# Seven products for one more pair in six tiles, strided units in halves, output products in another order

## The chip, the cores and the metric

The kernel runs on one core of one Trainium2 chip. The metric is device time in microseconds (us). In this text PE is TensorE's matmul stream, PEld its weight loads, DVE is VectorE, ACT is ScalarE, POOL is GpSimd and SP is SyncE. The program is scheduled by hand: each engine works through its own instructions in the order in which the kernel writes them, and semaphores tie the engines together.

## The reference, cut to what matters

Eight heads of attention feed a gated layer without an activation:

```
q, k, v: [8 batches, 8 heads, 576 positions, 64]
scores  = q k^T / 8
heads 0-3 keep 0 <= row - col < 32                      (local)
heads 4-7 keep row >= col and row % 32 == col % 32      (strided)
attn    = softmax(scores) v                             -> x: [8*576 tokens, 512]
a = x w_a ; b = x w_b                                   w_a, w_b: [512, 1536]
out = (a * b) w_out                                     w_out: [1536, 512]
```

Inputs and output are float32; the matmuls take bf16 and accumulate in float32.

## The kernel before, in words

**Tiles and slots.** The 4608 tokens are cut into nine tiles of 512, t = 0 to 8. (The short title of the change counts them from 1: its "tiles 3 to 7" are t = 2 to 6 here, and its "tile 8" is t = 7.) A tile has 16 slots. Slots 0 to 11 each make one of the twelve blocks of 128 hidden features: f = 0 to 11, or in pairs g = 0 to 5 with f = 2g and 2g + 1. Slots 12 to 15 are the output stage, which multiplies the hidden block `pf` by `w_out` and stores. While tile t runs, attention of batch b = t + 1 is threaded between its matmuls, at places that the tables STEPS, LATER, PAIRED, IN_P and IN_Y name. A table entry holds a position in the tile and what happens there: S0 to S7 (or s0 to s7 and m0 to m7, exponent and mask apart) are the scores of unit u = 0 to 7, V0 to V7 their products with v, Q0 to Q3 copies of q, O and I the way of the local heads through memory into `xT`. Units 0 to 3 are local heads, units 4 to 7 strided ones. `xT` is the attention output transposed, the right-hand side of the first matmuls; it holds four batches.

**A plain pair** (`ffn_ab`, L625): per block f, four matmuls of 512 columns for `a` and four for `b`; ACT copies `a` out (L646), DVE multiplies it by `b` into `pf` (L649).

**A pair by seven products** (`a_pair_mid` for t = 2 to 6, `a_pair` for t = 7 and 8): the `a` half of a pair is a two-by-two block product (two halves of the inner dimension, two blocks of features, two halves of the tokens), made of seven products instead of eight, each two matmuls of 256 columns. They work on sums of weights (`wsum_a`, DVE, L668) and of tokens (`xsum`, DVE, L678). ACT copies five results (L721, L724, L726, L731, L738), DVE adds three (L717). The `b` half stays at eight matmuls of 512 columns. The pair takes two slots; the first half of it ends at the first `yield`. Its order on PE, by the names in the code, is Y, X, three of b1, X again ("6"), Z ("7"), the last of b1 | X ("5"), Z ("4"), four of b0, X ("3"). After the bar comes the second slot. Steps listed at a slot's number are issued right behind that slot's matmuls. On DVE the second slot issues two additions, the step of IN_P, the third addition, then the two multiplies into `pf` (L714).

**The output stage** (`y_plan`, L895) uses the same seven-product form: fourteen groups of six matmuls of 256 columns, 84 in all, in the order Y_ORDER. A group is called by product and half, "60" for product 6 and half 0. Products 7, 6, 5 and 3 need sums over the hidden block, `ps` (`fast_s`, L829; n = 2, 1, 0, 3 in this order), which DVE makes from `pf`. ACT copies banks into `y_sb` (L860, L866), DVE adds (L858, L862, L864).

**PSUM banks.** From t = 2 on: three for `mm` and one for `tp` (dealt in turn by `mm_bank`), two for the scores `st`, one `o`, one `e`. `o` takes V0 to V3, and `o` and `e` together took the strided units 4 to 7. A bank can be written again only when its reader is done. For V0 to V3 the reader is DVE: a reciprocal (L468) and the normalising multiply (L486). For strided units (`step_VT`, L519 to L534) ACT makes the reciprocal of the row sums as exp(-ln) (L531, L532), then DVE multiplies into `xT` (L534).

**What is where before, in tiles 2 to 6.** Pairs 1 to 4 are by seven products, pairs 0 and 5 plain. V3 stands behind pair 3 (slot 7), S5's scores behind the first half of pair 4 (slot 8), V4 behind pair 4 (slot 9), S6's scores in pair 5, V5 behind it; S7, V6, V7 and the copies Q0, Q1 for the next batch lie in the output stage. In t = 7 pairs 1 to 5 are by seven products, in t = 8 all six.

Of the kernel before, what the change touches and what calls it, by code (L numbers as in the profile page):

```python
# [16 lines left out]
RS = 8  # L17
# [8 lines left out]
LV = 80  # L26
WCH = (0, 2, 5, 9, 12)
FAST_Y = (1, 2, 3, 4, 5, 6, 7, 8)
MID_A = {t: (1, 2, 3, 4) for t in (2, 3, 4, 5, 6)}
FAST_A = {7: (1, 2, 3, 4, 5), 8: (0, 1, 2, 3, 4, 5)}  # L30


@with_exitstack
def kernel(
# [473 lines left out]
    def step_VT(b, u):  # L508

        c, half, M, n, G = unit(u)  # L510
        p = ps.pop((b, u))
        if "e" in psum4:
            o = [psum4[nm].tile([128, 512], F32, tag=nm, name=nm) for nm in "oe"]
        else:
            o2 = psum4["o"].tile([128, 2, 512], F32, tag="o", name="o")
            o = [o2[:, j] for j in range(2)]
# [7 lines left out]
        if "e" not in psum4:  # L524
            by_j = lambda t: t.rearrange("d j (i p) -> d p i j", p=NP)
            nc.scalar.activation(by_token(r), by_j(o2[64:, :, :W]), ACT.Ln)
            nc.scalar.activation(r, r, ACT.Exp, scale=-1.0)
            nc.vector.tensor_mul(by_token(dst), by_j(o2[:64, :, :W]), by_token(r))
            return
        for j in range(2):  # L530
            nc.scalar.activation(by_token(r)[:, :, :, j], o[j][64:, :W].rearrange("d (i p) -> d p i", p=NP), ACT.Ln)  # L531
# [34 lines left out]
    def F_mm(f, w, kk):  # L566
# [115 lines left out]
    def a_pair_mid(t, g):  # L682
# [136 lines left out]
    def fast_s(t, n, gs):  # L819
        if t not in pss:  # L820
            pss[t] = nat.tile([128, FG * 5 * SW], BF16, tag="shared", name="ps").rearrange("p (n g m) -> p n g m", g=FG, n=5)
        s = pss[t][:, :, gs, :HT]
        x = pfs[t].rearrange("p (g e) (i m) -> p e i g m", e=2, i=2)[:, :, :, gs]
        a, b, op = ((x[:, 0, 1], x[:, 1, 1], ALU.add), (s[:, 0], x[:, 0, 0], ALU.subtract),
                    (x[:, 0, 0], x[:, 0, 1], ALU.subtract), (x[:, 1, 0], s[:, 1], ALU.subtract))[n]
        if (t, n) == (NT - 1, 2) and {gs.start, gs.start + 1} <= set(FAST_A[t]):
            later[t, gs.start] = lambda: nc.gpsimd.tensor_tensor(s[:, n], a, b, op=op)
            return
        nc.vector.tensor_tensor(s[:, n], a, b, op=op)  # L829
# [36 lines left out]
            nc.scalar.copy(part(0, 1), bank)  # L866
# [13 lines left out]
    def y_plan(t):  # L880

        plan, y = products(t), y_bufs()
        late = t in FAST_A
        if late:
            bank = {x: bank_of(nm, [128, 2, HN]) for x, nm in (("X", "mm"), ("Z", "mm"), ("Y", "tp"))}
        else:
            bank = {x: mm_bank([128, 2, HN]) for x in "ZXY"}

        def store_half(i):
            rows = out[TTOK * t:TTOK * (t + 1)].rearrange("(a i s q) c -> a s i (q c)", i=2, s=8, q=2)  # L890
            nc.sync.dma_start(out=rows[:, :, i], in_=y[i].rearrange("p q c -> p (q c)"))

        for k, q, g in by_block(Y_ORDER, 2 if late else 0):
            b, lhs, rhs = plan[k]
            nc.tensor.matmul(bank[b][:, q], lhsT=lhs(g, q), rhs=rhs(g), start=k in "172" and q == 0 and g == 0,  # L895
                             stop=g == FG - 1, skip_group_check=True)
# [54 lines left out]
    def ffn_y(t, j, mid):
        pf = pfs[t]
# [33 lines left out]
    with tc.manual_schedule(engines={ENG.PE, ENG.SP, ENG.Pool, ENG.DVE, ENG.Activation}):  # L986
# [76 lines left out]
        for t in range(NT):  # L1063
            slots += [(ffn_ab, t, f) for f in range(FD)] + [(ffn_ys if t in FAST_Y else ffn_y, t, j) for j in range(4)]
        for b in range(1, B):
            for pos, names in (STEPS.get(b) or {16 * (b - 1) + x: n for x, n in (PAIRED if b - 1 in MID_A else LATER).items()}).items():
                steps.setdefault(pos, []).append((b, names.split()))
            if b not in STEPS:
                for g in MID_A.get(b - 1, ()):
                    steps["p", b - 1, g] = [(b, IN_P[g].split())]  # L1070
                for n, names in IN_Y.items():
                    steps["y", b - 1, n] = [(b, names.split())]
# [107 lines left out]
```

## Time and profile before

| | us |
|---|---|
| three runs of the kernel | 318.88, 319.57, 321.58; median 319.57 |
| the profiled execution, its own time | 318.67 |
| its span (first to last instruction) | 317.0 |
| PE busy | 308.2 (97%) |
| DVE busy | 263.7 (83%) |
| ACT busy | 198.3 (63%) |
| POOL busy | 112.0 (35%) |
| one tile of t = 2 to 6, first to first matmul (tile 3: 123.05 to 155.93) | 32.88 |

The profiled execution spent 1.67 us outside its span. "Busy" of an engine joins overlapping instructions. A matmul of 512 columns is drawn as 0.38 us long, but the next one starts about 0.217 us later; so waits on PE are read from the distance of starts, not from gaps between bars. A timeline row merges equal instructions: its first number is the start of the first one, its second the time to the end of the last one, "x4" their number. A few matmul records are missing from the trace, and a row with fewer matmuls than the code issues has the same distance to the next row.

### The profile page before, as it was taken

What the parts mean: (1) busy time and instruction counts of PE and PEld (TensorE: products, weight loads), DVE (VectorE), ACT (ScalarE), POOL (GpSimd) and SP (SyncE); (2) the same over time, 40 slices, a digit from 0 to 9 for tenths busy, and PEclk for the clock granted to TensorE, in tenths of its full rate; (3) what the DMA queues carried; (4) which work ended last, traced back from release to release, by engine and by line L of the source; (5) the groups of instructions that cost most, each with busy time, mean ns of one, the idle gap of its engine ahead of it and who ended that gap; (6) DMA issues with size and microseconds to landing.
All of it is one profiled execution on the core that took longest, in us unless ns stands there. A gap on an engine that the chain in (4) does not pass through costs nothing. (4 is left out here: it accounts for less than half of the span.)

```text
span 317.0 us, 7353 instructions
## 1 busy us (share of the span) xinstructions
PE 308.2 (97%) x2770; PEld 220.6 (70%) x2798; DVE 263.7 (83%) x594; ACT 198.3 (63%) x414; POOL 112.0 (35%) x186
## 2 busy tenths in 40 slices
PE   7899999999999999999999999999999999999994
PEld 6754565455866687767999986769676966786684
DVE  6887876698979998999799978997899768847862
ACT  7964776455766776567666765686667755435541
POOL 8935712772263164115421434133101112203520
PEclk9999999999999999999999999999999999999999
DMA  9999999999799999999999999899352040004004
GB/s 159 168 205 202 203 184 202 216 104 172 127 137 148 223 144 81 127 228 134 108 114 225 118 130 106 202 138 134 30 154 58 0 135 0 2 0 133 2 0 134
DMA packets 127059, 40.32 MB, mean 127 GB/s; under 512 B 114864, under 2 KB 124144, under 8 KB 126832
## 3 DMA queue, kind: packets, MB, share of 16 engines
q0 software_dynamic: 79760, 19.20, 65.2%
q1 hardware_dynamic: 47120, 20.59, 38.8%
q8 instruction: 22, 0.36, 0.5%
q14 instruction: 13, 0.11, 0.1%
q10 hardware_dynamic: 144, 0.07, 0.1%
HBM read 38.93 MB, written 18.28 MB: 181 GB/s over the span
## 5 line engine op out<-in xcount | busy, mean ns | idle before, releaser
L625 PE MATMUL mm<-xT,wb_sb 128*128 128x512 bf16 (+1 forms) x189 | 46.8, 361 | 0.4
L625 PE MATMUL mm<-xT,wa_sb 128*128 128x512 bf16 (+1 forms) x183 | 46.1, 360 | 0.2
L1146 POOL CAST pace<-pf 1x1 f32<-1x1 bf16 x46 | 14.5, 316 | 81.1 <-DVE pf L714 31.6
L399 ACT ACTIVATE p<-st 72x576 bf16<-72x576 f32 (+1 forms) x56 | 36.4, 650 | 9.1 <-PE st L379 8.2
L709 PE MATMUL mm<-xT,wb_sb 128*128 128x512 bf16 (+1 forms) x160 | 38.0, 342 | 0.4
L646 ACT COPY a_sb<-mm 128x512 f32<-128x512 f32 x44 | 25.7, 583 | 15.7 <-PE mm L625 14.9
L895 PEld LDWEIGHTS <-ps 128*128 128x128 bf16 x336 | 32.7, 98 | 3.7
L625 PEld LDWEIGHTS <-wb_sb 128*128 128x128 bf16 x192 | 18.2, 98 | 16.8 <-DVE pf L714 0.3
L895 PE MATMUL mm<-wf,ps 128*128 128x256 bf16 x252 | 29.8, 273 | 0.0
L860 ACT COPY y_sb<-mm 128x512 f32<-128x512 f32 (+1 forms) x32 | 17.9, 558 | 19.0 <-PE mm L895 16.4
L649 DVE TENSOR_TENSOR pf<-a_sb,mm 128x512 bf16<-128x512 f32 x34 | 23.1, 680 | 5.9 <-ACT a_sb L646 5.8
L625 PEld LDWEIGHTS <-wa_sb 128*128 128x128 bf16 x192 | 17.4, 98 | 12.4
L1146 POOL COPY pace<-y_sb 1x1 f32<-1x1 f32 x22 | 8.4, 380 | 49.9 <-DVE y_sb L858 27.3
L895 PEld LDWEIGHTS <-pf 128*128 128x128 bf16 x252 | 23.5, 98 | 2.7
L775 PE MATMUL mm<-xT,wb_sb 128*128 128x512 bf16 x83 | 25.3, 379 | 0.1
L709 PEld LDWEIGHTS <-wb_sb 128*128 128x128 bf16 x192 | 18.7, 97 | 7.4
L238 POOL DMA_DIRECT2D vs<-in_v_dram x24 | 21.7, 907 | 3.9 <-ACT y_sb L860 1.3
L714 DVE TENSOR_TENSOR pf<-a_sb,mm 128x512 bf16<-128x512 f32 x35 | 22.7, 683 | 0.5
L895 PE MATMUL mm<-wo_sb,pf 128*128 128x256 bf16 x168 | 21.8, 273 | 0.0
L829 DVE TENSOR_TENSOR ps<-pf 128x512 bf16<-128x512 bf16 (+2 forms) x37 | 17.8, 481 | 0.7
L460 PEld LDWEIGHTS <-p 128*128 128x128 bf16 (+1 forms) x256 | 12.9, 97 | 5.2 <-DVE p L417 1.3
L417 DVE TENSOR_TENSOR p<-p,mask_l 128x576 int16<-128x576 int16 x32 | 14.4, 451 | 2.2 <-ACT p L399 2.0
(222 smaller groups left out, 734.2 us busy)
## 6 DMA issues: line engine op xcount, KB each, us to landing
out_dram<-y_sb SPq DMA_DIRECT2D x14, 512.0 KB, 4.8
kr<-in_k_dram POOLq DMA_DIRECT2D x12, 288.0 KB, 6.1
qr<-in_q_dram POOLq DMA_DIRECT2D x12, 288.0 KB, 8.1
vl<-in_v_dram POOLq DMA_DIRECT2D x6, 384.0 KB, 6.9
out_dram<-y_sb SPq DMA_DIRECT2D x7, 256.0 KB, 4.3
vs<-in_v_dram POOLq DMA_DIRECT2D x24, 72.0 KB, 5.7
xd<-xl SPq DMA_DIRECT2D x12, 144.0 KB, 4.0
wo_sb<-in_moe_w_out_dram POOLq DMA_DIRECT2D x4, 384.0 KB, 11.7
```

The lines of the kernel that those rows point to most:

```text
L238: nc.gpsimd.dma_start(out=vs_buf[b % 2][:, h, :, 0:D], in_=v[b, HL + h].rearrange("(p r) d -> p r d", r=RS))
L399: nc.scalar.activation(p_flat(p)[:M, :2 * W].rearrange("p (i n) -> p i n", n=2 * n), st[:M].rearrange("p a (i n) -> p (a i) n", n=256)[:, ...
L625: nc.tensor.matmul(ps_[:, c0:c0 + n], lhsT=w[:, kk, 128 * f:128 * (f + 1)], rhs=xT[:, kk, x0:x0 + n], start=(kk == first and c0 == 0), sto ...
L646: nc.scalar.copy(a_sb, ab[0])
L649: nc.vector.tensor_mul(pf[:, f, :].rearrange("p (i a s) -> p a i s", i=2, s=16), halves(a_sb), halves(ab[1]))
L709: nc.tensor.matmul(dst, lhsT=wb_sb[:, kk, 128 * f:128 * (f + 1)], rhs=rhs, start=kk == 0 and k in (None, 0), stop=kk == KD - 1 and k in (N ...
L714: nc.vector.tensor_mul(pf[:, 2 * g + e, :].rearrange("p (i a s) -> p a i s", i=2, s=16), halves(a[e]), halves(bank))
L775: nc.tensor.matmul(got[e], lhsT=wb_sb[:, kk, 128 * f:128 * (f + 1)], rhs=xT[:, kk, x0:x0 + TTOK], start=kk == 0, stop=kk == KD - 1)
L829: nc.vector.tensor_tensor(s[:, n], a, b, op=op)
L860: nc.scalar.copy({"1": part(0, 0), "7": part(0, 1), "6": part(1, 0), "5": part(1, 1)}[k], bank)
L895: nc.tensor.matmul(bank[b][:, q], lhsT=lhs(g, q), rhs=rhs(g), start=k in "172" and q == 0 and g == 0, stop=g == FG - 1, skip_group_check=True)
L1146: nc.gpsimd.tensor_copy(pace, done)
```

## The change

* In t = 2 to 6 pair 5 is made by seven products too, in t = 7 pair 0. Weight sums for group 5 are made together with those of groups 1 to 4.
* The strided units 4 to 7 of batches 3 to 7 are split by the parity of the positions. A half (`VT_p`) is four matmuls into one bank; one Ln and one Exp over 288 columns (`VT_x`) and one DVE multiply (`VT_n`) follow. Half 0 of unit 4 (`ua4`) and its half 1 (`ub4`) both use bank `o`; of units 5 to 7 half 0 uses `e` ("vc") and half 1 uses `o` ("vb").
* New places in the tile: s4's scores behind pair 2 (slot 5), s5's behind the first half of pair 3 (slot 6), `ua4` behind the first half of pair 4 (slot 8), s6's scores and `na4` behind pair 4 (slot 9), `ub4` behind the first half of pair 5 (slot 10), `nb4` behind pair 5. s7 and the halves of units 5 to 7 lie in the output stage at numbered matmuls of the 84 (IN_Y; for the last batch LAST_Y, with the halves sooner, and with `xsum` of t = 7 made there). Q0 and Q1 move to matmuls 47 and 60 of the output stage.
* The output products of t = 2 to 6 come in MID_ORDER, with the last block of the first three groups held back behind the first fifteen matmuls.
* The sums `ps` of these tiles are made in other portions: n = 2 in two parts, n = 1 in one (from n = 2 instead of n = 0), n = 0 and n = 3 in one each inside the output stage.

```diff
-MID_A = {t: (1, 2, 3, 4) for t in (2, 3, 4, 5, 6)}
-FAST_A = {7: (1, 2, 3, 4, 5), 8: (0, 1, 2, 3, 4, 5)}
+MID_A = {t: (1, 2, 3, 4, 5) for t in (2, 3, 4, 5, 6)}
+FAST_A = {7: (0, 1, 2, 3, 4, 5), 8: (0, 1, 2, 3, 4, 5)}
...
+    def VT_p(b, u, h, nm):
+        c, half, M, n, G = unit(u)
+        p = ps[b, u]
+        o = psum4[nm].tile([128, 512], F32, tag=nm, name=nm)
+        for i in range(G):
+            nc.tensor.matmul(o[:, i * n:(i + 1) * n], lhsT=vs_buf[b % 2][:, u - HL, 2 * i + h], rhs=p_cols(b, p, h, i, n, n)[:M],
+                             start=True, stop=True)
+        held[b, "vt", u, h] = o
+    def VT_x(b, u, h):
+        o = held[b, "vt", u, h]
+        r = sb.tile([128, RS * 4 * D], BF16, tag="xr", name="xr", bufs=2)[:64, :2 * W].bitcast(F32)
+        nc.scalar.activation(r, o[64:, :W], ACT.Ln)
+        nc.scalar.activation(r, r, ACT.Exp, scale=-1.0)
...
+    def VT_n(b, u, h):
+        o, r = held.pop((b, "vt", u, h))
+        by_token = lambda t: t.rearrange("d (i p) -> d p i", p=NP)
+        dst = xT[64 * (u % 2):64 * (u % 2) + 64, unit(u)[0], S * (b % XR):S * (b % XR + 1)]
+        nc.vector.tensor_mul(dst.rearrange("d (p i j) -> d p i j", i=4, j=2)[:, :, :, h], by_token(o[:64, :W]), by_token(r))
...
-    IN_Y = {2: "S7", 6: "V6", 11: "V7"}
-    PAIRED = {-4: "Q0", -3: "Q1", -1: "S0", 0: "S1", 1: "V0 Q2", 2: "s2", 3: "V1 Q3 O0", 4: "s3", 5: "V2", 6: "s4", 7: "V3 O1 I0", 8: "s5",
-              9: "V4 I1", 10: "s6", 11: "m6 V5"}
+    PAIRED = {-1: "S0", 0: "S1", 1: "V0 Q2", 2: "s2", 3: "V1 Q3 O0", 4: "s3", 5: "s4 V2", 6: "s5", 7: "V3 O1 I0", 8: "ua4",
+              9: "s6 na4 I1", 10: "ub4", 11: "nb4"}
     IN_P = {1: "m2", 2: "m3", 3: "m4", 4: "m5"}
+    IN_Q = {4: "ea4", 5: "eb4"}
+    IN_Y = {8: "vc5", 12: "s7", 14: "na5 m6", 24: "vb5", 26: "nb5 f0 m7", 34: "vc6", 36: "na6 f3", 44: "vb6", 46: "nb6", 56: "vc7",
+            58: "na7", 67: "vb7", 69: "nb7"}
+    LAST_Y = {8: "vc5", 12: "s7", 14: "na5 m6", 24: "vb5", 26: "nb5 m7", 32: "vc6", 34: "na6 f0", 40: "vb6", 42: "nb6", 50: "vc7",
+              52: "na7 f3", 60: "vb7", 62: "nb7", 63: "x0 x1 x2 x3"}
...
         nc.scalar.copy(quarter(1, 1), X)
+        take(("q", t, g))
...
-        if g == 4:
-            fast_s(t, 0, slice(0, 4))
...
+        if n == 1 and t in MID_A:
+            a, b = x[:, 1, 1], s[:, 2]
...
+    MID_ORDER = [(x[0], int(x[1])) for x in "10 11 20 70 71 60 61 40 41 50 51 21 30 31".split()]
...
-        for k, q, g in by_block(Y_ORDER, 2 if late else 0):
+        for m, (k, q, g) in enumerate(by_block(MID_ORDER, 3) if t in MID_A else by_block(Y_ORDER, 2 if late else 0)):
...
+            take(("m", t, m + 1))
...
-            do((17, 17, 18, 19)[n], wsum_make, n, slice(1, 5))
-            do(16 * 2 + 12 + n, wsum_make, n, slice(0, 6, 5))
+            do((17, 17, 18, 19)[n], wsum_make, n, slice(1, 6))
+            do(16 * 2 + 12 + n, wsum_make, n, slice(0, 1))
...
-        do(16 * (NT - 2) - 1, xsum_make, NT - 2, 0)
-        for n in (2, 1, 3):
-            do(16 * (NT - 2), xsum_make, NT - 2, n)
```

More of the change, by code (lines that the diff above doesn't have):

```diff
@@ L511, in step_VT @@
         p = ps.pop((b, u))
[L512 to L516, printed above, removed]
+        o2 = psum4["o"].tile([128, 2, 512], F32, tag="o", name="o")
+        o = [o2[:, j] for j in range(2)]
         for j in range(2):
@@ L523, in step_VT, with VT_px @@
         dst = xT[64 * (u % 2):64 * (u % 2) + 64, c, S * (b % XR):S * (b % XR + 1)]
[L524 to L531, printed above, removed]
-        nc.scalar.activation(r, r, ACT.Exp, scale=-1.0)
-        for j in range(2):
-            nc.vector.tensor_mul(by_token(dst)[:, :, :, j], o[j][:64, :W].rearrange("d (i p) -> d p i", p=NP),
-                                 by_token(r)[:, :, :, j])
+        by_j = lambda t: t.rearrange("d j (i p) -> d p i j", p=NP)
+        nc.scalar.activation(by_token(r), by_j(o2[64:, :, :W]), ACT.Ln)
+        nc.scalar.activation(r, r, ACT.Exp, scale=-1.0)
+        nc.vector.tensor_mul(by_token(dst), by_j(o2[:64, :, :W]), by_token(r))
+    def VT_p(b, u, h, nm):
[11 more added lines that the diff above has]
+        nc.scalar.activation(r, r, ACT.Exp, scale=-1.0)
+        held[b, "vt", u, h] = o, r
+    def VT_px(b, u, h, nm):
+        VT_p(b, u, h, nm)
+        VT_x(b, u, h)
+    def VT_n(b, u, h):
[3 more added lines that the diff above has]
+        nc.vector.tensor_mul(dst.rearrange("d (p i j) -> d p i j", i=4, j=2)[:, :, :, h], by_token(o[:64, :W]), by_token(r))
     def X_p(b, c):
@@ L584 @@
                  30: "V7"}}
-    LATER = {-4: "Q0", -3: "Q1", -1: "S0", 0: "S1", 1: "V0", 2: "S2", 3: "V1 Q2 O0", 4: "S3 Q3", 5: "V2", 6: "S4", 7: "V3 O1 I0", 8: "S5", 9: "V4 I1",
-             10: "S6",
-             11: "V5"}
-    IN_Y = {2: "S7", 6: "V6", 11: "V7"}
-    PAIRED = {-4: "Q0", -3: "Q1", -1: "S0", 0: "S1", 1: "V0 Q2", 2: "s2", 3: "V1 Q3 O0", 4: "s3", 5: "V2", 6: "s4", 7: "V3 O1 I0", 8: "s5",
-              9: "V4 I1", 10: "s6", 11: "m6 V5"}
-    IN_P = {1: "m2", 2: "m3", 3: "m4", 4: "m5"}
+    PAIRED = {-1: "S0", 0: "S1", 1: "V0 Q2", 2: "s2", 3: "V1 Q3 O0", 4: "s3", 5: "s4 V2", 6: "s5", 7: "V3 O1 I0", 8: "ua4",
+              9: "s6 na4 I1", 10: "ub4", 11: "nb4"}
+    IN_P = {1: "m2", 2: "m3", 3: "m4", 4: "m5"}
+    IN_Q = {4: "ea4", 5: "eb4"}
[3 more added lines that the diff above has]
+              52: "na7 f3", 60: "vb7", 62: "nb7", 63: "x0 x1 x2 x3"}
     FN = {"Tk": step_Tk, "Tq": step_Tq, "S": step_S, "V": step_V, "X": step_X, "W": lambda b, n: fast_w(n, slice(0, 3)),
-          "s": S_px, "m": S_m, "L": lead_vl, "O": rows_out, "I": rows_in, "Pk": lambda b, c: pair_up("k", c), "Pq": lambda b, c: pair_up("q", c),
+          "s": S_px, "m": S_m, "ua": lambda b, u: VT_p(b, u, 0, "o"), "ub": lambda b, u: VT_p(b, u, 1, "o"),
+          "ea": lambda b, u: VT_x(b, u, 0), "eb": lambda b, u: VT_x(b, u, 1),
+          "vc": lambda b, u: VT_px(b, u, 0, "e"), "vb": lambda b, u: VT_px(b, u, 1, "o"), "na": lambda b, u: VT_n(b, u, 0), "nb": lambda b, u: VT_n(b, u, 1),
+          "f": lambda b, n: fast_s(b - 1, n, slice(0, FG)), "x": lambda b, n: xsum_make(b, n), "L": lead_vl, "O": rows_out, "I": rows_in, "Pk": lambda b, c: pair_up("k", c), "Pq": lambda b, c: pair_up("q", c),
           "Q": lambda b, n: step_Q(b, n // 2, n % 2)}
@@ L948, in ffn_ys @@
                 pass
-        return (y[0][:1, 0, :1], None, y[1][:1, 0, HN:HN + 1], y[1][:1, 0, :1])[j]
+        ends = y[1][:1, 0, HN:HN + 1], y[1][:1, 0, :1]
+        return (y[0][:1, 0, :1], None, *(ends[::-1] if t in MID_A else ends))[j]
     def ffn_y(t, j, mid):
@@ L1065 @@
         for b in range(1, B):
-            for pos, names in (STEPS.get(b) or {16 * (b - 1) + x: n for x, n in (PAIRED if b - 1 in MID_A else LATER).items()}).items():
+            t = b - 1
+            for pos, names in (STEPS.get(b) or {16 * t + x: n for x, n in PAIRED.items()}).items():
                 steps.setdefault(pos, []).append((b, names.split()))
             if b not in STEPS:
[L1069 to L1072, printed above, removed]
+                for kind, where in (("p", IN_P), ("q", IN_Q), ("m", LAST_Y if b == B - 1 else IN_Y)):
+                    for x, names in where.items():
+                        steps.setdefault((kind, t, x), []).append((b, names.split()))
+                for x, pos, nm in ((28, 47, "Q0"), (29, 60, "Q1")):
+                    steps.setdefault(("m", t - 1, pos) if t - 1 in MID_A else x, []).append((b, [nm]))
         at = {}
@@ L1080 @@
         for t in FAST_Y[:-1]:
+            if t in MID_A:
+                continue
             if t not in FAST_A:
@@ L1130 @@
             for slot, n, z0, z1 in (
-                    ((8, 0, 0, 4),) if t == 1 else ()) + ((9, 2, 0, 4), (10, 1, 0, 4), (12, 3, 0, 6)) if t == 1 or t in MID_A else ((4, 0, 0, 2), (5, 2, 0, 2), (6, 1, 0, 2), (7, 3, 0, 2), (8, 2, 2, 4), (9, 0, 2, 4),
+                    (8, 0, 0, 4), (9, 2, 0, 4), (10, 1, 0, 4), (12, 3, 0, 6)) if t == 1 else (
+                    (9, 2, 0, 4), (11, 2, 4, 6), (11, 1, 0, 6)) if t in MID_A else ((4, 0, 0, 2), (5, 2, 0, 2), (6, 1, 0, 2), (7, 3, 0, 2), (8, 2, 2, 4), (9, 0, 2, 4),
                                     (10, 1, 2, 4), (12, 3, 2, 6)):
```

## The prediction

> **What bounds the kernel.** I read the page's shares first, then the windows of one tile, then the timeline of PE and DVE inside it. Part 1 and the clock:
>
> ```profile
> PE 308.2 (97%) x2770; PEld 220.6 (70%) x2798; DVE 263.7 (83%) x594; ACT 198.3 (63%) x414; POOL 112.0 (35%) x186
> ...
> PEclk9999999999999999999999999999999999999999
> ```
>
> The windows of tile 3, hidden slots and output stage (PE, PEld, DVE, ACT, POOL busy):
>
> ```profile
> 123.05:145.98 22.93, 22.77 (x184) 14.67 (x185) 22.02 (x52) 15.20 (x35) 7.86 (x12) 1.00 1.20 151
> 145.98:155.93 9.95, 9.95 (x111) 9.01 (x107) 8.41 (x18) 7.17 (x14) 3.61 (x8) 1.00 1.83 127
> ```
>
> PE is full. DVE comes next with 22.02 + 8.41 = 30.4 of 32.88 us. The timeline of PE shows a plain block:
>
> ```profile
> 142.01 1.03 PE L625 MATMUL mm<-xT,wa_sb 128*128 128x512 bf16 x4
> 142.88 1.03 PE L625 MATMUL mm<-xT,wb_sb 128*128 128x512 bf16 x4
> 143.74 0.41 PE L379 MATMUL st<-qz0s,kT0s 128*128 128x144 bf16 x4
> ```
>
> Four matmuls take 0.87 us from start to start, 0.217 each. I compared all starts from 60 us on with such pitches (256 columns 0.109, a score unit 0.25, a local V 0.18, half a strided unit 0.13): one distance behind 90 us is longer without a missing record, 0.24 us at 284.5. So whatever the change takes from PE, or makes it wait, is time, one for one.
>
> **The gain.** A plain pair is 4 x 0.866 = 3.46 us of PE (142.01 to 145.72 without the scores). Pair 2 by seven products runs from 130.87 to 134.37 with 0.25 of scores inside: 3.25. That is 0.21 a pair, six pairs: **-1.3 us**. Nothing else leaves PE; the halves are the same eight matmuls as a whole unit.
>
> **A new wait for bank `o`, slot 8.** This decides my forecast. Around pair 3, PE and then DVE:
>
> ```profile
> 137.84 0.38 PE L695 MATMUL mm<-xT,tq 128*128 128x256 bf16 x2
> 138.06 0.34 PE L460 MATMUL o<-vl,p 128*128 128x65 bf16 x6
> 138.24 0.60 PE L695 MATMUL mm<-xT,wa_sb 128*128 128x256 bf16 x4
> ...
> 139.98 0.41 PE L379 MATMUL st<-qz0s,kT0s 128*128 128x144 bf16 x4
> ```
>
> ```profile
> 137.96 0.41 DVE L717 TENSOR_TENSOR a_sb<-p,a_sb 128x256 f32<-128x256 f32 x1
> 138.41 0.69 DVE L714 TENSOR_TENSOR pf<-a_sb,e 128x512 bf16<-128x512 f32 x1
> 139.01 0.68 DVE L714 TENSOR_TENSOR pf<-a_sb,mm 128x512 bf16<-128x512 f32 x1
> 139.61 0.18 DVE L468 RECIPROCAL rc<-o 96x6 f32<-96x6 f32 x1
> 139.83 0.55 DVE L486 TENSOR_TENSOR xl<-o,rc 96x384 bf16<-96x384 f32 x1
> ```
>
> V3 fills `o` at 138.06. DVE comes to V3 only behind the two multiplies of pair 3, and leaves `o` at 139.83 + 0.55 = 140.38. Before, PE put scores into another bank at 139.98, and nobody needed `o`. The change puts `ua4` exactly there, and it writes `o`; the built program has it wait for that L486. Everything behind it on PE waits too. The release takes another 0.05 (in the timeline an L486 ends at 17.00 and PE follows at 17.05), so PE stops from 139.98 to 140.43, 0.45 us; if the weight load (98 ns, page) has to follow the wait, 0.55. In tiles 2, 4, 5 and 6 the L486 starts at 107.02, 172.80, 205.74, 238.62 and the scores at 107.11, 172.97, 205.90, 238.77: 0.51, 0.43, 0.44 and 0.45 by the same sum. Together 2.3 us, with the weight loads 2.8. [...] I take **+2.5**.
>
> DVE can't be earlier: its chain from product "4" (addition, mask, addition, two multiplies, reciprocal, multiply) has no idle time in this pair, and the change leaves it as it is up to there.
>
> **Smaller waits at pair 5.** Behind pair 4 come s6's scores and at once pair 5. With pair 4's last product ended at 0, ACT copies it out at 0.20 (138.26 against 138.06), starts the exponent of s6 at 0.47 and is free 0.55 later, at 1.02 (starts 136.74 and 137.29). So the first copy of pair 5 runs to 1.39, and product "6" into the same bank, due at 0.25 + 0.43 + 0.65 = 1.33, comes at about 1.44: 0.1. `ub4` waits for `na4`, which DVE reaches at 1.55 (143.30 against 141.75) and ends, at 0.47 like L534, at 2.02; with the release 2.07, due on PE at 0.25 + 1.74 + 0.1 = 2.09: nothing to 0.1. Five times 0.12: **+0.6** (0 to 1.0).
>
> **Output stage of tiles 2 to 6.** From its start at 0, DVE ends pair 5's multiplies at about 1.2, the sums n = 2 and n = 1 (starts of neighbours 0.34 and 0.86 apart, as such rows show) at 3.0; product "60" comes at 0.25 + 0.26 + 30 x 0.109 = 3.8. Then na5, m6, nb5 (behind ACT's Ln and Exp), n = 0 at 5.4 against 6.7 for "50"; n = 3 at 7.0 against 8.9 for "30"; nb7 at 10.3 against 11.6, when the next tile needs the last quarter of `xT`; the last addition at 10.9 against 12.3, when its bank is needed. So moved masks, halves, Q0 and Q1 are hidden behind output matmuls, with 0.6 to 1.8 us to spare. In tile 2 four short weight sums take 0.7 of that. One place is tight: "30" needs the copy of "51", and only "21" (0.65) and a half unit (0.13) lie between, against 0.20 + 0.58 + 0.05 for the copy (149.05 and its kind): 0.05 each, **+0.2** with what else is late by a hair (0 to 0.5).
>
> An Exp over 288 columns has no row. Copies of 256 and 512 columns take 0.37 and 0.58, Ln over 288 0.42 to 0.44, Exp over 576 0.68; I take 0.42, between 0.37 and 0.58. [...]
>
> **From tile 6 to tile 7: +0.6.** The last batch's order has n = 3 behind na7, which waits for ACT; I get about 12.45 for its end where "30" comes at 12.3: 0.1 to 0.3. Pair 0 of tile 7 is now by seven products, and its first copy stands behind the copy of the last output bank. That case is in the trace, at the start of tile 8:
>
> ```profile
> 283.82 0.58 ACT L866 COPY y_sb<-mm 128x512 f32<-128x512 f32 x1 [2.04 <-PE mm L895]
> 284.30 0.38 ACT L784 COPY a_sb<-ax 128x256 f32<-128x256 f32 x1
> 284.73 0.38 PE L768 MATMUL ax<-qz1s,tq 128*128 128x256 bf16 x2
> ```
>
> PE was due at 284.49: 0.24, which tile 7 now has as well. Third, b0 of that pair needs the bank that DVE frees with the last output addition, which now stands behind four token sums (0.34 each): 0 to 0.3. Bounds 0.24 to 1.0.
>
> At nothing: weight sums of group 5 (same elements in fewer instructions, and tile 1 has no PE wait); three more additions per tile on DVE (0.34 each, less 0.3 from fewer sums: 31.2 of some 33 us); one more ACT copy and four more Exp per tile (ACT has 10 us idle). If DVE's cover goes, that is the second rival.
>
> **Sum.** -1.3 + 2.5 + 0.6 + 0.2 + 0.6 = +2.6 us on the profiled execution's 318.67 (span 317.0 and 1.67 around it): 321.3. Its time lies 0.9 under the median of the runs shown, 319.57; I put the forecast between the two bases at **321.7**. The terms' ends give -1.3 + 2.3 + 0 + 0 + 0.24 = +1.2 and -1.3 + 2.8 + 1.0 + 0.5 + 1.0 = +4.0.
>
> **Rivals.**
> 1. *The waits are not there, the pairs pay.* If `o` were free in time, by a DVE some 0.5 us earlier, only -1.3 + 0.24 to 0.6 remains: about 317.8 on the profiled base, 318.7 on the median. For it: PE has no wait of this kind now. Against: the order on DVE and the rows above. 0.10.
> 2. *DVE becomes the bound.* The multiplies of half units read the reciprocals in another order than L534 did, which no row shows. If each took 0.68, as multiplies of 512 columns do, instead of 0.47, eight would cost 1.7 us a tile and DVE would need 32.9, more than PE's 32.67 without waits. It decides once DVE enters the output stage over 0.8 us late: "60" and "70" then wait for their sums, about 0.4 us in each of five tiles on top: +4.6, 323.3 on the profiled base, 324 on the median. For it: 93% busy. Against: the same strided output as L534. 0.20.
> 3. *The seven products don't shorten a pair*, because 256-column matmuls wait for weight loads: excluded, for pair 2 shows 3.25 us.
>
> **Numbers.** Forecast 0.65, first rival 0.10, second 0.20, anything else 0.05. About 1% (3.2 us) is what a measurement of this kernel can tell from no change. Faster by that: 0.02, since all gains are 1.3 us. Slower by that: the second rival and the forecast's upper end, 0.27. Within: 0.71. Range 319.3 to 324.0: from the forecast's lower end to the second rival.
>
> **What would show it.** In tiles 2 to 6 of the changed kernel PE starts `ua4` 0.45 to 0.55 us late, right behind the normalising multiply of V3; "6" of pair 5 0.1 late; no wait from "10" to "51"; tile 7's first "6" 0.24 late; a pair 5 of 3.25 us without waits. I would be wrong if DVE reached V3 earlier than 1.5 us behind pair 3, or if the sums for "60" and "70" came late.

## The result, and the profile after

The changed kernel took **327.7 us** (median of five runs, 327.28 to 330.37), against 319.57 before: a ratio of 1.027, 95% interval 1.020 to 1.033. The forecast was 321.7 with a range of 319.3 to 324.0, so the sign was right and the size was not: 8.1 us were added, not 2.1. The profiled execution of the changed kernel took 330.37 us, with a span of 328.6. Three single executions in a slower state (331.58 and 326.62 us of two variants, 324.75 us of the kernel before) are left out of the medians and ratios below.

Part 1 of its page and the clock:

```profile
PE 315.5 (96%) x2826; PEld 223.6 (68%) x2826; DVE 277.1 (84%) x601; ACT 206.4 (63%) x452; POOL 113.9 (35%) x184
...
PEclk9999999999999999999999999999999979999999
```

PE's share hardly moves, since the whole span grew with it; the one "7" of the clock row will matter below. To see where the time lies, I compared the starts of the output stages, in the timeline of PE, from stage to stage (us):

| from output stage to output stage | before | after | difference |
|---|---|---|---|
| span's start to tile 0 | 42.06 | 43.23 | +1.17 |
| 0 to 1 | 38.09 | 38.55 | +0.46 |
| 1 to 2 | 32.95 | 33.44 | +0.49 |
| 2 to 3 | 32.88 | 34.40 | +1.52 |
| 3 to 4, 4 to 5, 5 to 6 | 33.03, 32.88, 32.88 | 33.94, 33.81, 33.83 | +0.91, +0.93, +0.95 |
| 6 to 7 | 29.68 | 34.70 | +5.02 |
| 7 to 8 | 28.94 | 29.10 | +0.16 |
| 8 to the end | 13.6 | 13.6 | 0.0 |

The first row isn't the change: in the profiled executions of eight of the ten variants below the first output stage starts at 42.0 to 42.7, and this execution waited for its loads longer (PE 0.9 us at one place, for a load of q). About half of the rest lies in one place, the passage from tile 6 to tile 7.

**Tile 3, by windows** (hidden slots and output stage; PE, PEld, DVE, ACT, POOL busy, clock), the rows that answer to the two before, from the score unit with which the tile begins:

```profile
126.18:149.62 23.44, 23.06 (x183) 14.88 (x182) 22.24 (x53) 15.38 (x38) 7.69 (x12) 1.00 1.18 148
149.62:160.19 10.57, 10.46 (x114) 9.20 (x112) 10.34 (x18) 8.54 (x19) 4.21 (x9) 1.00 1.63 117
```

In the output stage DVE was busy for 8.41 of 9.95 us before and is for 10.34 of 10.57 now. That is the row which says that DVE has next to nothing to spare there any more.

**The wait for bank `o`**, timeline of PE and DVE around the second half of pair 4, tile 3:

```profile
143.16 0.18 DVE L468 RECIPROCAL rc<-o 96x6 f32<-96x6 f32 x1
...
143.32 0.38 PE L731 MATMUL mm<-xT,wb_sb 128*128 128x512 bf16 x1
143.38 0.55 DVE L486 TENSOR_TENSOR xl<-o,rc 96x384 bf16<-96x384 f32 x1
...
144.08 0.29 PE L532 MATMUL o<-p,vs 72*128 72x72 bf16 x4 [0.38 <-DVE xl L486]
144.21 0.38 PE L717 MATMUL mm<-xsum,tk 128*128 128x256 bf16 x2
```

A matmul of 512 columns at 143.32 makes the next one due at 143.54, 0.217 later by the pitch. `ua4` comes at 144.08, 0.54 late, 0.15 behind the end of V3's L486 at 143.93. The same 0.53 to 0.54 stands in all of tiles 2 to 6. This was the step that decided the forecast. The wait is there, and its length is at the upper end of what I had given.

**The passage from tile 6 to tile 7**, timeline of DVE, ACT and PE:

```profile
261.74 0.63 DVE L553 TENSOR_TENSOR xT<-o,xr 64x288 bf16<-64x288 f32 x1
262.40 0.43 DVE L700 TENSOR_TENSOR qz1l<-xT 128x512 bf16<-128x512 bf16 x1
...
262.70 0.81 PE L796 MATMUL mm<-xT,wb_sb 128*128 128x512 bf16 x3
...
263.54 0.42 DVE L700 TENSOR_TENSOR qz1l<-xT,qz1l 128x512 bf16<-128x512 bf16 x1
263.88 0.69 DVE L881 TENSOR_TENSOR y_sb<-y_sb 128x512 f32<-128x512 f32 x1
...
264.65 0.58 ACT L889 COPY y_sb<-mm 128x512 f32<-128x512 f32 x1 [3.59 <-DVE y_sb L881]
265.13 0.38 ACT L805 COPY a_sb<-ax 128x256 f32<-128x256 f32 x1
265.56 0.46 PE L789 MATMUL ax<-qz1l,tq 128*128 128x256 bf16 x2 [2.05 <-ACT a_sb L805]
```

Read it from the bottom. PE's product "6" of tile 7's first pair waits 2.21 us beyond its pitch for the copy L805. That copy stands on ACT behind L889, the copy of the last output bank, and L889 had waited 3.59 us: it writes the part of `y_sb` that the addition "+" (L881) still has to read. And "+" stands on DVE behind the last multiply of the halves and four token sums (L700), which the new order put there. Before, at the same place, "+" (L858) ran 2.3 us ahead of the last copy (L866), which waited for PE alone:

```profile
252.65 0.69 DVE L858 TENSOR_TENSOR y_sb<-y_sb 128x512 f32<-128x512 f32 x1
...
254.92 0.58 ACT L866 COPY y_sb<-mm 128x512 f32<-128x512 f32 x1 [0.65 <-PE mm L895]
```

In the changed kernel the list of waits has the wait for "+" in every tile of 2 to 6 (first line; the other two are `ua4` and `ub4`):

```profile
ACT y_sb L889 <- DVE y_sb L881: 9.1, 5, 3.6
...
PE o L532 <- DVE xl L486: 1.9, 5, 0.4
PEld L532 <- DVE xT L553: 1.8, 5, 0.4
```

(The columns are the total, the times and the longest.) In tiles 2 to 5 it is shorter (1.24 to 1.80), the next tile begins with plain blocks, and PE shows no wait for that copy.

**Half clock behind the gap.** The windows of the stretch that follows, with the granted clock in the last but two columns:

```profile
265.50:267.00 1.50, 1.44 (x7) 0.92 (x7) 0.00 (x0) 0.47 (x3) 0.00 (x0) 0.58 0.37 85
267.00:269.00 2.00, 2.00 (x9) 1.09 (x8) 0.42 (x1) 0.65 (x2) 0.72 (x1) 0.50 0.98 287
```

From 265.8 to 269.2 the matmuls come at double distance, 0.43 us for two of 256 columns instead of 0.22; by the sum of the excesses that is another 1.6 us. The slow stretch lasted 3.4 us, and the gap in front of it 2.2 us; why the clock fell and came back isn't shown. Not every execution shows this: of the five, three had a mean clock of 0.998 to 1.0. They took 327.28 to 327.7, the median, at 1.0, is one of them, and it carries the gap without the slow stretch.

**Three smaller waits.** In the output stage of tile 3 the half unit `vc6` waits for its mask (timeline):

```profile
150.84 0.66 DVE L553 TENSOR_TENSOR xT<-o,xr 64x288 bf16<-64x288 f32 x1
...
152.76 1.26 PE L919 MATMUL mm<-wf,ps 128*128 128x256 bf16 x10
152.85 0.64 DVE L553 TENSOR_TENSOR xT<-e,xr 64x288 bf16<-64x288 f32 x1
...
153.52 0.46 DVE L417 TENSOR_TENSOR p<-p,mask_s 72x576 int16<-72x576 int16 x1
...
154.12 0.29 PE L532 MATMUL e<-p,vs 72*128 72x72 bf16 x4
```

Ten matmuls of 0.109 make `vc6` due at 153.85; the mask m6 ends at 153.98, and PE follows at 154.12, 0.26 late (0.49 in tile 6). Ahead of that mask lie multiplies of half units at 0.64 to 0.66 us. The same operation in the kernel before, and now, in the views of one line (min/median/max in ns):

```profile
L534 DVE TENSOR_TENSOR xT<-o,xr x20: 470/476/481, 111.0 to 254.3; 64x288 bf16<-64x288 f32 x20
```

```profile
L553 DVE TENSOR_TENSOR xT<-o,xr x25: 627/642/660, 112.9 to 261.7; 64x288 bf16<-64x288 f32 x25
```

Same shape, same types: 0.17 us more each. `ub4` also comes 0.15 late at pair 5, behind `na4`, which takes 0.63. In tile 1, PE waits 0.49 for the mask of V0, with weight sums of 0.82 ahead of it on DVE (0.68 before, four of them), and before the change there was no wait at that place:

```profile
66.22 0.82 DVE L690 TENSOR_TENSOR tq<-wa_sb,tq 128x1280 bf16<-128x1280 bf16 x1
...
68.02 0.45 DVE L417 TENSOR_TENSOR p<-p,mask_l 128x576 int16<-128x576 int16 x1
68.53 0.35 PE L460 MATMUL o<-vl,p 128*128 128x65 bf16 x6 [0.33 <-DVE p L417]
```

### The profile page after: what moved, and what is told of

The parts are those of the page before. It is cut to its first block, busy times and chain, and to the rows that moved or that the text cites. A ratio compares the mean times of both kernels' runs of the same rounds, so it can differ in the third digit from the quotient of the medians.

```text
span 328.6 us, 7523 instructions
## 1 busy us (share of the span) xinstructions
PE 315.5 (96%) x2826; PEld 223.6 (68%) x2826; DVE 277.1 (84%) x601; ACT 206.4 (63%) x452; POOL 113.9 (35%) x184
## 4 chain that ended last, share of the span: by engine, by line
PE 79%; DVE 9%; DMA 5%; issue 2%; ACT 2%; POOL 1%; DVEq 0%; POOLq 0%; ACTq 0%
PE mm L919 15%; PE mm L647 14%; PE mm L731 9%; PE mm L717 6%; PE mm L796 6%; DMA vl<-in_v_dram 5%; PE st L379 4%; PE e L717 4%; PE ax L789 3%; PE mm L983 3%; PE mm L789 3%; PE o L460 2%; DVE pf L736 2%; PE mm L947 2%; PE o L532 1%
## 5 line engine op out<-in xcount | busy, mean ns | idle before, releaser
L1174 POOL CAST pace<-pf 1x1 f32<-1x1 bf16 x41 | 16.1, 393 | 76.8 <-DVE pf L736 40.3
L647 PE MATMUL mm<-xT,wa_sb 128*128 128x512 bf16 (+1 forms) x136 | 34.7, 366 | 0.0
L919 PE MATMUL mm<-wf,ps 128*128 128x256 bf16 x252 | 32.1, 273 | 0.0
L736 DVE TENSOR_TENSOR pf<-a_sb,mm 128x512 bf16<-128x512 f32 x45 | 29.3, 684 | 0.7
L796 PE MATMUL mm<-xT,wb_sb 128*128 128x512 bf16 x96 | 29.3, 387 | 0.0
L668 ACT COPY a_sb<-mm 128x512 f32<-128x512 f32 x32 | 18.7, 583 | 11.3 <-PE mm L647 11.0
L647 PEld LDWEIGHTS <-wa_sb 128*128 128x128 bf16 x136 | 12.4, 98 | 9.6
L541 ACT ACTIVATE xr<-xr 64x288 f32<-64x288 f32 x40 | 17.8, 444 | 1.3
L671 DVE TENSOR_TENSOR pf<-a_sb,mm 128x512 bf16<-128x512 f32 x22 | 15.0, 681 | 3.7 <-ACT a_sb L668 3.6
L852 DVE TENSOR_TENSOR ps<-pf 128x512 bf16<-128x512 bf16 (+3 forms) x32 | 17.0, 531 | 0.5
L739 DVE TENSOR_TENSOR a_sb<-mm,a_sb 128x256 f32<-128x256 f32 x40 | 16.1, 415 | 1.0 <-PE mm L717 0.7
```

The lines of the kernel that those rows point to most:

```text
L647: nc.tensor.matmul(ps_[:, c0:c0 + n], lhsT=w[:, kk, 128 * f:128 * (f + 1)], rhs=xT[:, kk, x0:x0 + n], start=(kk == first and c0 == 0), sto ...
L668: nc.scalar.copy(a_sb, ab[0])
L736: nc.vector.tensor_mul(pf[:, 2 * g + e, :].rearrange("p (i a s) -> p a i s", i=2, s=16), halves(a[e]), halves(bank))
L796: nc.tensor.matmul(got[e], lhsT=wb_sb[:, kk, 128 * f:128 * (f + 1)], rhs=xT[:, kk, x0:x0 + TTOK], start=kk == 0, stop=kk == KD - 1)
L1174: nc.gpsimd.tensor_copy(pace, done)
```

## The experiments

My theory after the two traces (A): PE is full, so each of these waits is time by itself, and taking away what makes it gives back its length. The rivals are named with each run: a wait that only moves, or lateness that DVE keeps whatever is repaired. Each run was compared with the kernel before on the same chip; the medians of before were 319.07 for the first four variants, 319.4 for the next four and 318.96 for the last two. Where times of different groups are set side by side, differences of half a microsecond say nothing by themselves; there the distances in the traces decide.

### V3 in another bank

V3 writes into the scores' bank, so `ua4` finds `o` free.

```diff
-                o = psum4["o"].tile([128, 512], F32, tag="o", name="o")
+                o = (pst.tile([128, 2, 512], F32, tag="st", name="o")[:, 0] if u == 3 else
+                     psum4["o"].tile([128, 512], F32, tag="o", name="o"))
```

> V3 of batches 3 to 7 writes into the scores' bank, which is free at that point, instead of bank o; all else as in the changed kernel (median 327.7 us). Theory A, the waits are local and add up: PE no longer stands 0.54 us in front of ua4 in each of tiles 2 to 6, no other wait grows, and the time falls by 2.7 us to about 325.0; the distance from one output stage to the next falls from 33.8 to 33.3 us. Theory B, DVE is the bound and the place of the wait is chance: the 0.54 us come back at ub4 and in the output stage, and the time falls by less than 1 us.

Measured: 327.53 us, 1.026 (1.019 to 1.033), where 325.0 was expected. Locally it did what it should; timeline of tile 3 at the same place, DVE and then PE:

```profile
142.04 0.55 DVE L487 TENSOR_TENSOR xl<-o,rc 96x384 bf16<-96x384 f32 x1
```

```profile
141.98 0.38 PE L732 MATMUL mm<-xT,wb_sb 128*128 128x512 bf16 x1
142.19 0.29 PE L533 MATMUL o<-p,vs 72*128 72x72 bf16 x4
142.38 0.38 PE L718 MATMUL mm<-xsum,tk 128*128 128x256 bf16 x2
142.66 0.38 PE L718 MATMUL e<-xsum,wa_sb 128*128 128x256 bf16 x2
```

`ua4` starts 0.21 behind the matmul ahead of it, without waiting for the multiply at 142.04. The distances between output stages fell from 34.40, 33.94, 33.81, 33.83 to 33.97, 33.52, 33.35, 33.38: 0.42 to 0.46 each, not 0.54. The rest shows in these rows: the half unit takes 0.19 and the two matmuls behind it 0.28, where the waiting one took 0.13 and 0.22. Here the half unit behind a 512-column matmul costs about 0.11 more when it doesn't wait. The median didn't follow, since the gap at tile 7 and the half clock behind it were still there: all four runs had a mean clock of 0.988 to 0.994 and lay between 326.1 and 330.2. The effect is measured without them further down.

### Token sums behind the addition "+"

```diff
-              52: "na7 f3", 60: "vb7", 62: "nb7", 63: "x0 x1 x2 x3"}
+              52: "na7 f3", 60: "vb7", 62: "nb7", 66: "x0 x1 x2 x3"}
```

> In the output stage of tile 6 the four token sums for tile 7 are issued behind the addition that reads the bank of product 5, not ahead of it. Theory A: the copy of the last output bank no longer waits for that addition behind four sums, ACT goes on to the first copy of tile 7 at once, the PE wait of 2.2 us at the start of tile 7 falls to about 0.25, and with it goes the stretch at half clock behind it; the distance from output stage 6 to output stage 7 falls from 34.7 us to about 31, the time by 2 us against executions without the half clock (325.5) and by more against those with it. Rival: the wait is DVE's backlog as a whole, whatever the order; then the distance stays above 33.5 us.

Measured: 326.04 us (325.88 to 326.08), 1.020 (1.016 to 1.025). Timeline at the start of tile 7:

```profile
261.30 0.69 DVE L881 TENSOR_TENSOR y_sb<-y_sb 128x512 f32<-128x512 f32 x1
...
262.08 0.59 ACT L889 COPY y_sb<-mm 128x512 f32<-128x512 f32 x1 [2.13 <-DVE y_sb L881]
...
262.56 0.38 ACT L805 COPY a_sb<-ax 128x256 f32<-128x256 f32 x1
...
262.99 0.38 PE L789 MATMUL ax<-qz1l,tq 128*128 128x256 bf16 x2 [0.58 <-ACT a_sb L805]
```

"+" now runs right behind the last multiply, and the same chain ends 1.47 us sooner: PE's wait falls from 2.21 to 0.74, not to the 0.25 that I expected. No half clock follows. The distance from tile 6 to 7 is 31.59 instead of 34.70, which leaves the rival out. So the order of two groups of instructions on DVE, not their amount, made most of the gap. The rest goes with the other repairs: in the profiled executions further down the 0.74 is 0.49 with the reading order added, and 0.24, as at the start of tile 8, with everything repaired.

### Reciprocals in the order in which they are read

ACT writes the logarithms by token, and the multiply then reads them as one run; nothing else changes.

```diff
-        nc.scalar.activation(r, o[64:, :W], ACT.Ln)
+        nc.scalar.activation(r.rearrange("d (p i) -> d p i", i=4), o[64:, :W].rearrange("d (i p) -> d p i", p=NP), ACT.Ln)
...
-        nc.vector.tensor_mul(dst.rearrange("d (p i j) -> d p i j", i=4, j=2)[:, :, :, h], by_token(o[:64, :W]), by_token(r))
+        nc.vector.tensor_mul(dst.rearrange("d (p i j) -> d p i j", i=4, j=2)[:, :, :, h], by_token(o[:64, :W]), r.rearrange("d (p i) -> d p i", i=4))
```

> The reciprocals of a half unit are written by Ln in token order and read by the DVE multiply in that order; the same work otherwise. Theory A: the multiply takes 0.64 us instead of 0.47 because it reads its float32 reciprocals across 288-byte steps; it falls back to 0.47, DVE gains some 1.4 us a tile, the waits at ub4 (0.15) and in front of unit 6 in the output stage (0.26) go, in five tiles 1.8 us, to about 325.9. Rival: the length comes from something else in the instruction, it stays near 0.64 us and the time near 327.7.

Measured: 324.98 us (324.89, 324.98 and 328.01), 1.020 (1.013 to 1.027). ACT's logarithm takes 0.41 us in the run with all repairs, as in the changed kernel. The multiply is back where L534 was, in the view of its line:

```profile
L553 DVE TENSOR_TENSOR xT<-o,xr x25: 465/478/484, 111.7 to 258.2; 64x288 bf16<-64x288 f32 x25
```

`ub4`'s wait and `vc6`'s are gone in tiles 2 to 5, and so are the extra waits of tile 2. The distances are 33.47, 33.59, 33.49, 33.48. The gap at tile 7 stayed, 1.95 us.

### All of these, and two smaller repairs

The three edits together; in the last batch `f3` before `na7` (at 48 and 52); the weight sums of group 5 made apart, behind tile 1's attention:

```diff
-            do((17, 17, 18, 19)[n], wsum_make, n, slice(1, 6))
+            do((17, 17, 18, 19)[n], wsum_make, n, slice(1, 5))
+            do(28 + n, wsum_make, n, slice(5, 6))
```

> The three edits together, with n = 3 of the last batch two places earlier and the weight sums of group 5 moved from the start of tile 1 into its output stage. Theory A, local waits that add up: 2.7 + 2.0 + 1.8 + 0.4 + 0.4 us less than the changed kernel, about 320.4, with 0.1 at pair 5 and 0.25 at the start of tile 7 left on PE. Theory B, DVE as the bound: the sum of the gains is less than two thirds of that, above 323.

Measured: 320.59 us, 1.005 (1.003 to 1.008). The changed kernel lay 8.1 us above the kernel before, this one lies 1.5 above it: some 6.6 us come back by removing waits that the traces had named. What is left: tiles 2 to 6 at 33.05 (one at 33.17) from output stage to output stage against 32.88 (one at 33.03) before, and 30.78 against 29.68 from tile 6 to 7. The 0.17 of a tile is -0.21 for the pair, +0.09 for the late "6" of pair 5, +0.22 for two half units that now don't wait and cost 0.11 each as above, and 0.07 in pieces that I didn't follow.

### Pair 0 of tile 7 plain again

```diff
-FAST_A = {7: (0, 1, 2, 3, 4, 5), 8: (0, 1, 2, 3, 4, 5)}
+FAST_A = {7: (1, 2, 3, 4, 5), 8: (0, 1, 2, 3, 4, 5)}
```

> The changed kernel with pair 0 of tile 7 made plain again, nothing else. Theory A: the 2.21 us wait at the start of tile 7 exists because product "6" of that pair needs a bank whose copy (ACT L805) stands behind the last output copy (L889), which waits for the addition "+"; a plain pair writes other banks first and doesn't need that copy for some 2 us. Then the wait of 2.2 and the half clock behind it are gone, the pair costs 0.21 more, and the median goes from 327.4 to about 325.4. Rival: the gap is made by the output stage itself (DVE late with its sums and additions); then the plain pair stands for as long, and the median stays at 327.4 to 327.9.

Measured: 326.04 us (325.8 to 326.14), 1.018 (1.009 to 1.026). Between the two expectations. The half clock is gone, but a wait stays:

```profile
263.12 0.69 DVE L887 TENSOR_TENSOR y_sb<-mm,y_sb 128x512 f32<-128x512 f32 x1
263.29 0.58 ACT L889 COPY y_sb<-mm 128x512 f32<-128x512 f32 x1 [3.58 <-DVE y_sb L881]
...
263.93 1.02 PE L647 MATMUL mm<-xT,wa_sb 128*128 128x512 bf16 x4 [0.91 <-ACT y_sb L889]
```

The plain blocks run for 1.7 us more, and then the third of them needs the bank that the late copy L889 reads: 1.07 us late. So the pair in seven products wasn't the cause, only the place where the cause was felt first. The larger part of the cause is "+" behind the token sums, as the run with the sums moved had shown; my theory had the plain pair hide the wait whole, and it hides half.

### The bank and the reading order again, without the gap

Two runs combine one edit each with the token sums behind "+", so that they are read against 326.04 (measured in the other group) and against that run's distances.

```diff
+                o = (pst.tile([128, 2, 512], F32, tag="st", name="o")[:, 0] if u == 3 else
...
+              52: "na7 f3", 60: "vb7", 62: "nb7", 66: "x0 x1 x2 x3"}
```

> V3 written into the scores' bank, together with the token sums behind the addition "+": to be read against the kernel with the token sums alone (326.04), since neither has the long wait and the half clock that hid the effect before. Theory A (ua4's wait is lost time, one for one): five waits of 0.54 go, and a half unit that doesn't wait costs 0.11 more than one that does (0.19 + 0.28 us in the trace instead of 0.13 + 0.22), so 326.04 - 5 x 0.43 = 323.9. Rival: the time comes back at the next tight place of the pair or of the output stage; then 325.5 or more.

```diff
+        nc.scalar.activation(r.rearrange("d (p i) -> d p i", i=4), o[64:, :W].rearrange("d (i p) -> d p i", p=NP), ACT.Ln)
...
+              52: "na7 f3", 60: "vb7", 62: "nb7", 66: "x0 x1 x2 x3"}
```

> Reciprocals stored in the order in which the multiply reads them (multiply 0.48 instead of 0.64 us), together with the token sums behind the addition "+"; to be read against the token sums alone, 326.04. Theory A (the eight slow multiplies a tile make DVE late and cost PE 0.3 to 0.4 us in each of five tiles, and 0.6 more in tile 2): about 324.1. Rival: DVE's time is hidden and the shorter distances seen before were shifts between stages; then 325.7 or more.

Measured: 323.9 us, 1.012 (1.005 to 1.019), for the bank, and 323.41, 1.011 (1.003 to 1.019), for the reading order. The bank gave 2.1 us, five times 0.43, as expected. The reading order gave 2.6, with distances of 33.48, 33.58, 33.49 and 33.47; I had expected 1.9. In the trace 0.54 of it lies from tile 6 to 7 (31.05 instead of 31.59), where I had counted a part of that. Both rivals (the time comes back elsewhere) fall.

### A version meant to beat both

V3's bank and the reading order, pair 0 of tile 7 plain, the order of tiles 2 to 5 for tile 6 too (no special order for the last batch), weight sums of group 5 in tile 2, and:

```diff
-              9: "s6 na4 I1", 10: "ub4", 11: "nb4"}
+              9: "na4 I1", 10: "s6"}
...
-    IN_Q = {4: "ea4", 5: "eb4"}
-    IN_Y = {8: "vc5", 12: "s7", 14: "na5 m6", 24: "vb5", 26: "nb5 f0 m7", 34: "vc6", 36: "na6 f3", 44: "vb6", 46: "nb6", 56: "vc7",
+    IN_Q = {4: "ea4"}
+    IN_Y = {4: "ub4 eb4", 8: "vc5", 12: "s7", 13: "nb4", 14: "na5 m6", 24: "vb5", 26: "nb5 f0 m7", 34: "vc6", 36: "na6 f3", 44: "vb6", 46: "nb6", 56: "vc7",
```

> All repairs, and three more: pair 0 of tile 7 plain with the order of tiles 2 to 5 in the output stage of tile 6; weight sums of group 5 in tile 2's plain blocks instead of tile 1; ub4 and its multiply moved from pair 5 into the output stage, s6's scores behind the first half of pair 5. From the 320.4 of the earlier repaired kernel: tile 6 to 7 gives 1.1, tile 1 0.35, and pair 5's late "6" (0.09) and one of the two slow half units (0.11) 0.2 in each of five tiles: 318.0 if all of it holds. Rival: ub4 in the output stage makes DVE late with the sums for "60" and "70", 0.4 us in each of five tiles: 320 or more.

Measured: 320.88 us, 1.004 (1.000 to 1.007). A miss: 318.0 was expected. The rival came nearer, though not by its mechanism: "60" and "70" weren't late. Without s6's scores between pairs 4 and 5, the first matmuls of pair 5's b1 come 0.25 earlier than before, and wait 0.19 for a bank whose copy isn't done; in the output stage `vb5` waits 0.11 for `nb4` (0.36 in tile 4). A tile takes 33.14 to 33.38. Read from the rows alone, the scores had been the cover for that copy (L762, whose end, 143.49, is where b1 starts, 143.55). That is an argument, no run put other work there. The weight sums cost more at one place: in tile 2 they stand between the additions of pairs 2 and 3 on DVE, PE waits 0.17, 0.10 and 0.34 there, and from output stage 1 to 2 this kernel takes 33.20, against 32.73 in the next one, which makes the same sums in tile 1. As hoped, `ub4` behind 256-column matmuls took 0.13, without the excess.

### The repairs that held, and pair 5 taken out of them

The second last kernel keeps V3's bank, the reading order and the weight sums behind tile 1, leaves `ub4` and s6 in pair 5, and has the plain pair 0 of tile 7 with the order of tiles 2 to 5 in tile 6. The last one makes pair 5 of tiles 2 to 6 plain as well (`eb4` then stands right behind `ub4`).

```diff
-                for kind, where in (("p", IN_P), ("q", IN_Q), ("m", LAST_Y if b == B - 1 else IN_Y)):
+                for kind, where in (("p", IN_P), ("q", IN_Q), ("m", IN_Y)):
...
+        do(16 * (NT - 2) - 1, xsum_make, NT - 2, 0)
+        for n in (2, 1, 3):
+            do(16 * (NT - 2), xsum_make, NT - 2, n)
```

> The repairs that held (V3 in the scores' bank, reciprocals in reading order, weight sums of group 5 behind tile 1's attention), ub4 back in pair 5, and instead of the special order for the last batch the order of tiles 2 to 5, with pair 0 of tile 7 plain. Theory: from the 320.4 of the earlier repaired kernel the distance from tile 6's output stage to tile 7's falls from 30.78 to about 29.85 and the next from 29.10 to 28.95: 319.3, level with the kernel before. Rival: the first blocks of tile 7 still stand behind the last output copy, 1 us as when only pair 0 was undone: 320.3.

```diff
-MID_A = {t: (1, 2, 3, 4, 5) for t in (2, 3, 4, 5, 6)}
+MID_A = {t: (1, 2, 3, 4) for t in (2, 3, 4, 5, 6)}
```

> The same kernel with pair 5 of tiles 2 to 6 plain again, so that the halves of the strided units stand alone. Theory: pair 5 by seven products takes 0.21 less of PE and costs 0.09 by its late product "6", so the plain pair is 0.12 longer in each of five tiles: 0.6 us more than the kernel it is compared with, about 319.9. Rival: the pair gives nothing by itself once everything else waits less (DVE makes three additions more for it): the same or less than 319.3.

Measured: 319.64 us, 1.000 (0.997 to 1.004), for the first, near the theory's 319.3, and 320.76, 1.004 (1.000 to 1.007), for the last. Part 1 of the first one's page:

```profile
PE 309.7 (97%) x2788; PEld 223.9 (70%) x2820; DVE 270.2 (85%) x603; ACT 206.2 (65%) x449; POOL 114.0 (36%) x185
```

With most of its waits gone and without its pair 0 of tile 7, the change is level with the kernel before, and no better: tile 6 to 7 now takes 30.00, 7 to 8 28.94, tiles 2 to 6 still 33.05. The plain pair 5 lengthens a tile by 0.10 to 0.18, near the 0.12 expected; its `ub4` waits 0.09 to 0.18 in its turn. Five tiles make some 0.65 of the 1.1 between the medians, whose intervals overlap, so the medians alone settle nothing. That pair 5 by seven products gives something is shown by the traces, tile by tile. It gives less than the rest of the change costs: with the plain pair 5 a tile takes 33.15 to 33.36, against 32.88 and 33.03 before. How much of that is the half units and how much the new order isn't shown.

## Why the prediction was wrong, and where it was right

**Right: the gain.** Pair 5 of tile 3 starts at 145.98 and ends at 149.62; without the half unit (0.13) and its two waits (0.10 and 0.15) that is 3.26 us, as forecast from pair 2 (3.25).

**Right: the wait of `ua4`, mis-sized in one piece.** Forecast 2.5 us, 0.43 to 0.55 a tile; 0.54 a tile, 2.7. The 2.5 lay between my two sums, 2.3 and 2.8, and no run shows that figure. My reason for the upper end was a weight load of 98 ns that has to follow the wait. The row of the weight loads (PEld) doesn't bear it out:

```profile
144.05 0.19 PEld L532 LDWEIGHTS <-vs 72*128 72x128 bf16 x4 [0.74 <-issue]
```

The load starts 0.12 behind the end of L486, and the first matmul 0.03 behind the start of the load. So the load does follow the wait, but the matmul isn't drawn as waiting for the whole load. What I had too short is the release, 0.05 taken and 0.15 measured. Where the 0.1 more comes from stays open. Taking the wait away gave 2.1 of the 2.7, for the reason that the half unit then costs 0.11 more.

**Mis-sized: the waits at pair 5.** The late "6" is 0.09 to 0.10 (forecast 0.1). For `ub4` I had "nothing to 0.1", with `na4` "at 0.47 like L534"; at 0.63 it is 0.15. Together 1.2 us instead of 0.6.

**Failed: the output stage of tiles 2 to 6, "hidden behind output matmuls, with 0.6 to 1.8 us to spare".** Two faults. First, it took the multiplies at 0.47; the run with the reciprocals rewritten showed that their reading order alone makes them 0.64. My second rival had named precisely this ("in another order", 0.68, eight a tile) and I gave it 0.20, because the output of L534 is strided too; that was the wrong operand to look at. Second, the list of deadlines had sums and additions in it but not `vc6`, which needs the mask m6: 0.26 in tiles 2 to 5, 0.49 in tile 6. The rival's own price (late "60" and "70") didn't come; the lateness came out at the next place that was tight. Together with tile 2, where weight sums come on top, the output matmuls and the waits among them take 1.8 us more in tiles 2 to 5.

**Failed, and the largest: "From tile 6 to tile 7: +0.6."** I had seen the four token sums ahead of the last addition, and priced them only for the bank that b0 needs (0 to 0.3). I took the first copy of tile 7 to be 0.24 late behind the last output copy, as at the start of tile 8, without asking what that copy itself waits for. It waits for "+", which had moved behind nb7 and the token sums. So the step that failed is the wait that I took from the start of tile 8. Measured: 2.21 us at "6", 0.48 at "30" (forecast 0.1 to 0.3), 0.49 at `vc6`, and 1.6 of half clock in the profiled execution. The move of the sums alone gave back 1.5 of the 2.21 in the trace, and 1.7 between the medians.

**Failed: weight sums of group 5 "at nothing", since "tile 1 has no PE wait".** Five groups instead of four make each sum 0.82 instead of 0.68, and the mask of V0 comes 0.49 late; with the group made elsewhere this wait is gone. Nor was it true that tile 1 had no PE wait: the trace of before has 0.28 and 0.09 there, at 71.48 and 73.75, and the repaired kernel has them too. PE waited for masks of DVE (L417) there already.

**The small price.** Exp over 288 columns: taken 0.42, measured 0.44 to 0.45 (L541). It had no part in the miss.

By the terms: -1.3 + 2.7 + 1.2 + 1.8 + 1.1 (waits in tile 6's output stage) + 2.2 + 0.5 (tile 1) + 0.2 (tile 7 to 8) = 8.4. The span grew by 11.6, of which 1.2 is the late start and 1.6 the half clock; 0.4 of the 8.8 that remain is in pieces that I didn't follow. The last row but one of the table, 0.16 from tile 7 to 8, disappears with tile 7's plain pair 0 and was not followed either.

## What to carry to other kernels

On an engine that works in order, price a moved group of instructions by everything that stood behind it, followed to the end: the four sums moved ahead of "+" cost nothing on DVE, and 1.5 us two engines further on. When an instruction's duration is taken from its like, compare how each operand is laid out, inputs as well as output. Before counting a wait as gone, ask what covered it: here a plain pair, and as it seems a set of scores between two pairs, hid a late copy, and both times removing the cover let it out.

## What the runs showed of the hardware

**Reading order.** A DVE multiply of 64x288 float32 took 0.64 us when its second input was read with steps of 72 elements, and 0.48 when it was one run; with steps of two elements, in the kernel before, it took 0.46 to 0.48. The difference between 0.64 and 0.48 is 0.57 ns an element. Three layouts were measured, and no row of the kernel before has the one with the long steps; why it costs more isn't shown.

**Clock.** A gap of 2.2 us in PE's work was followed by about 3.4 us of matmuls at double distance in the profiled execution of the changed kernel, with a granted clock of 0.50 from 267 to 269, and in that of the kernel with V3 in another bank, whose mean clock was 0.994. Behind gaps of 1.95 us (reading order alone) and 1.07 us (plain pair 0 of tile 7) the granted clock stayed at 1.00, and behind 0.74 us (sums moved, mean clock 1.0) two matmuls of 256 columns went on taking 0.22. These are single executions, so no limit follows from them. Nor does every slow stretch stand behind such a gap: in two profiled executions (all repairs; reading order with the sums moved) matmuls came at double distance for 6.8 us near the start, from 16.4 and 15.8 us on, and PE's longest gaps before that were 1.25 and 0.85 us; the mean clocks were 0.989 and 0.987. The stretch at tile 7 cost 1.6 us, on top of the 2.2 of the gap ahead of it.

**A short weight-loading group.** Four matmuls of 72 columns cost 0.13 us behind the 256-column matmuls of the output stage or after a wait, and 0.24 with what follows them when they come without a wait behind the single 512-column matmul that ends the first half of a pair by seven products. The width of the matmul ahead isn't the reason: in tile 4 of the run with all repairs two matmuls of 256 columns stand in its place, and the half unit at 177.30 and the matmuls behind it take 0.18 and 0.28, as behind the 512-column one; and in the kernel before, the eight matmuls of V5, straight behind the four 512-column matmuls of a plain block (145.72 to 145.98), cost 0.13 for each four. Why is open.
